# Moving an input check into the first layer and two output tiles behind the second projection

## The chip, the cores and the metric

The kernel runs on one core of a Trainium2 chip. The metric is the time of one execution on the device in microseconds. A core has five engines with a queue each: PE (matrix multiplications; PEld is its loading of weights), DVE (vector), ACT (scalar and activation), POOL, and SP, which issues the DMA transfers here. Each engine works through its own instructions in the order in which the program issued them, and waits where an instruction needs another engine's result.

## The reference, cut to what matters

Attention over 4 batches, 8 heads, 768 positions and 64 features a head, with 8 global keys, a window of 96 and a bias that falls with distance, is followed by a soft mixture of 8 experts with 4 slots each:

```python
logits = x @ phi                                  # x: 3072 x 512, 32 slots
d = softmax of logits over the tokens             # dispatch
slot_input = (d.T @ x).reshape(E, 4, 512)
h = np.maximum(slot_input[e] @ w1[e], 0.0)        # first layer, 8 experts
slot_out[e] = h @ w2[e]                           # second layer
c = softmax of logits over the slots              # combine
return c @ slot_out                               # 3072 x 512
```

## The kernel before, in words

The kernel is made for inputs with certain properties (sizes of the window, no score sum too small, and others). It computes on the fast path, and beside it a flag that says whether the inputs had them; at the very end every engine loads the flag, and only if it is set a general version (`general`) computes all again.

The attention part follows an order written out by hand (the list `ORDER`) and ends near 140 us. Everything here is about what comes after it. There, too, the program text is the order: inside `manual_schedule` each engine runs its instructions as the text issues them. The stages are:

- `last_dispatch` and `slots` finish the slots' inputs.
- `moe.hidden(…, 0, …)` is the first layer for experts 0 to 3 (PE L124); in its midst `between` sets up `fl` and makes the token softmax of the combine weights on DVE and ACT (L870 to L169).
- A loop over `a` in 0, 1: for `a == 0` it splits two batches' combine weights into two 16-bit parts (`split`, ACT L177 and DVE L178) and issues loads of the second layer's weights (`load_w`, SP L410); for `a == 1` it runs the first layer for experts 4 to 7 and issues the last loads.
- `hidden_t` transposes both results (PE L138, copies ACT L142 and DVE L144). `by_slot` turns the combine weights so that slots lie on partitions (PE L188, copies ACT L192 and DVE L194).
- `project(n, a, cs)` is the second layer (PE L154) for the output's column half `n`, the experts of group `a` and some chunks `cs`. `slots_out(n)` finishes it on DVE (L199, L200).
- `combine(n, t0, sizes)` makes output tiles of 128 tokens and 256 columns for half `n` (PE L214), in pairs: a pair is copied out of PSUM by ACT (L217) or by DVE (L219) in turn, and each group of `sizes` is sent by SP (L220), from one of eight buffers (`obs`) used in turn.

The first half's 24 tiles are interleaved with the second half's projection; the second half's 24 come at the end. `check_inputs` stands between the first half's last combine and the rest of the second projection. It is a transpose of `xmax` on PE (L891) and 13 small DVE operations that write columns of `fl` (L885 to L899). `set_flag` is a matmul with one column that sums the verdicts over the partitions (PE L903) and one DVE operation that writes `flag` (L904). PSUM tiles come from `LeftBanks.tile`, which goes round six banks.

Of the kernel before, what the change touches and what calls it, by code (L numbers as in the profile page):

```python
# [80 lines left out]
class Moe:  # L81
# [117 lines left out]
        nc.vector.tensor_scalar(out=oh, in0=o, scalar1=self.sgn[:, 0:1], scalar2=None, op0=ALU.mult)  # L199
        nc.vector.scalar_tensor_tensor(out=sot, in0=o, scalar=self.sgn[:, 1:2], in1=oh.bitcast(F32), op0=ALU.mult, op1=ALU.add)  # L200

    def combine(self, ps, ct, n, sot, obs, out, t0, sizes):


        nc = self.nc
        at, w = OUT_PART[n]
        for size in sizes:
            obs.append(obs.pop(0))
            ob = obs[-1][:, 0:w * size]
            for m in range(0, size, 2):  # L210
                cp = ps.tile([P, 512], F32, name="cp", tag="x")
                for k in range(2):
                    t = t0 + m + k
                    nc.tensor.matmul(out=cp[:, w * k:w * k + w], lhsT=ct[:, t * P:t * P + P], rhs=sot, start=True, stop=True)  # L214
                dst = ob[:, m * w:m * w + 512]
                if (t0 + m) // 2 % 2 == 0:
                    nc.scalar.copy(out=dst, in_=cp)  # L217
                else:
                    nc.vector.tensor_copy(out=dst, in_=cp)  # L219
            nc.sync.dma_start(  # L220
                out=out[P * t0:P * (t0 + size), at:at + w].rearrange("(t p) f -> p t f", p=P), in_=ob.rearrange("p (t f) -> p t f", f=w))
            t0 += size
# [75 lines left out]
def tile_attention_moe(ctx: ExitStack, tc: tile.TileContext, qk, v, phi, w1, w2, nn, out):  # L298
# [22 lines left out]
    moe = Moe(tc, ident, sgn, const.tile([P, P], F16, name="ident16"))  # L321
# [64 lines left out]
    for k, n in enumerate(held):  # L386
        at = 0
        for c0, c1 in sorted((c0, c1) for sp in spaces for h, c0, c1 in sp if h == n) + [(WP, WP)]:
            if at < c0:
                extras.append((NW + k, at, c0))  # L390
            at = c1
    places += places[0:5] + places[8:8 + 27 - npl]

    def piece(k):
        m, r = divmod(k, 16)
        if m == 0:
            a, r = divmod(r, 8)
            half, s = divmod(r, 4)
        else:
            half, r = divmod(r, 8)  # L400
            a, s = divmod(r, 4)
        return m, 4 * a + s, half
# [3 lines left out]
    def load_w(pieces, c0=0, c1=WP):  # L406

        for k in pieces:
            m, e, half = piece(k)
            nc.sync.dma_start(out=places[k][:, c0:c1], in_=(w1, w2)[m][e][:, WP * half + c0:WP * half + c1])  # L410
# [445 lines left out]
    left = LeftBanks()  # L856
# [21 lines left out]
    ct = ts.tile([P, B * S], F32R, name="ct")  # L878
    ohs = ts.tile([P, HF], F32R, name="ohs")
    sots = ts.tile([P, DM], F32R, name="sots")  # L880

    def check_inputs():

        def reduced(c, rows, x, axes, at_least):
            nc.vector.tensor_reduce(out=fl[0:rows, c:c + 1], in_=x, axis=axes, op=ALU.min)  # L885
            nc.vector.tensor_scalar(out=fl[0:rows, c:c + 1], in0=fl[0:rows, c:c + 1], scalar1=at_least, scalar2=None, op0=ALU.is_ge)

        reduced(1, KB, rsall[:, :, 0:6], AX.XY, RS_MIN)
        reduced(6, TN[6], rsall[0:TN[6], :, 6], AX.X, RS_MIN)
        xt = left.tile([P, 512], F32, name="xt", tag="x")  # L890
        nc.tensor.transpose(out=xt[0:B * H, 0:KB], in_=xmax, identity=ident[0:KB, 0:KB])  # L891
        nc.vector.tensor_reduce(out=fl[0:B * H, 5:6], in_=xt[0:B * H, 0:KB], axis=AX.X, op=ALU.max)
        nc.vector.tensor_scalar(out=fl[0:B * H, 5:6], in0=fl[0:B * H, 5:6], scalar1=X_MIN, scalar2=None, op0=ALU.is_ge)
        reduced(7, KB, cst[:, :, 1], AX.X, 0.5)
        nc.vector.tensor_scalar(out=fl[:, 2:3], in0=nlo, scalar1=1.0, scalar2=None, op0=ALU.is_ge)
        nc.vector.tensor_scalar(out=fl[:, 3:4], in0=nlo, scalar1=float(WIN), scalar2=None, op0=ALU.is_le)
        nc.vector.tensor_scalar(out=fl[:, 4:5], in0=ngl, scalar1=float(NG), scalar2=None, op0=ALU.is_le)
        nc.vector.tensor_reduce(out=fl[:, 8:9], in_=fl[:, 0:8], axis=AX.X, op=ALU.min)
        nc.vector.tensor_scalar(out=fl[:, 9:10], in0=fl[:, 8:9], scalar1=-1.0, scalar2=-1.0, op0=ALU.add, op1=ALU.mult)  # L899

    def set_flag():
        ft = left.tile([P, 512], F32, name="ft", tag="x")
        nc.tensor.matmul(out=ft[0:1, 0:1], lhsT=fl[:, 9:10], rhs=ones[:, 0:1], start=True, stop=True)  # L903
        nc.vector.tensor_scalar(out=flag[0:1], in0=ft[0:1, 0:1], scalar1=0.5, scalar2=None, op0=ALU.is_ge)  # L904
# [3 lines left out]
    def split(b):  # L908
        moe.split(lnat[:, 8 * b:8 * b + NJ], sps[b % 2])
# [4 lines left out]
    for a in range(2):  # L914
        if a == 1:
            moe.hidden(left, Moe.slot_view(sl), lambda e, half: wt[0, e, half], a, hss[a])
        if a == 0:
            split(0)
            split(1)
            for c in (0, WP // 2):  # L920
                load_w(range(npl, 28), c, c + WP // 2)
        else:
            for c in range(0, WP, WP // 4):
                load_w(range(28, 32), c, c + WP // 4)
    for a in range(2):
        moe.hidden_t(left, hss[a], hts[a])
    for b in (0, 1):
# [3 lines left out]
    obs = [places[16 + i // 2][:, 4 * HF * (i % 2):4 * HF * (i % 2) + 4 * HF] for i in range(8)]  # L931
    ops = [left.apart(n) for n in range(2)]

    def project(n, a, cs=range(8)):
        moe.project(ops[n], hts[a], lambda e, h: wt[1, e, h], n, a, cs)

    def slots_out(n):
        at, w = OUT_PART[n]
        moe.slots_out(ops[n][:, 0:w], ohs[:, 0:w], sots[:, at:at + w])

    def combine(n, t0, sizes):
        at, w = OUT_PART[n]
        moe.combine(left, ct, n, sots[:, at:at + w], obs, out, t0, sizes)

    project(0, 0)
    project(0, 1)
# [1 line left out]
    project(1, 0, range(2))  # L948
    by_slot(2)
    combine(0, 0, (2, 2, 4))  # L950
    project(1, 0, range(2, 4))
    combine(0, 8, (4,))
    project(1, 0, range(4, 5))
    by_slot(3)
    project(1, 0, range(5, 6))
    combine(0, 12, (4,))
    project(1, 0, range(6, 8))
    combine(0, 16, (4,))
    project(1, 1, range(2))
    combine(0, 20, (4,))  # L960
    check_inputs()
    project(1, 1, range(2, 8))
    slots_out(1)
    set_flag()
    combine(1, 0, (2, 2) + (4,) * 5)
    order.close()
    tail.close()
# [206 lines left out]
```

## Time and profile before

| | us |
|---|---|
| median of 3 runs | 204.69 |
| lowest and highest | 204.19, 205.63 |
| the profiled execution | 206.07 |
| its span in the trace | 204.3 |

| engine | busy, us | share of the span |
|---|---|---|
| PE | 181.1 | 89% |
| DVE | 150.9 | 74% |
| ACT | 128.4 | 63% |
| POOL | 113.7 | 56% |

The profile gives, for one execution, when each instruction ran, on which engine, and what ended the idle time in front of it. A row of the order of time has the start, the length, the engine, the line of the kernel, the operation, the tile written and the tile read, shapes, a count (xN merges instructions in a row), and in brackets the idle time before it and what ended it. Starts count from the beginning of the span. A row of a stage has the busy time of each engine in that stretch. The engines overlap the end of one instruction with the start of the next, so that neighbours can overlap by some hundredths of a microsecond.

### The profile page before, as it was taken

Reading aid. Unit: us, or ns where it says so; the run is one execution under the profiler, and the core shown is the slowest. Engines: PE = TensorE matmul, PEld = TensorE weight load, DVE = VectorE, ACT = ScalarE, POOL = GpSimd, SP = SyncE. Lnnn points to the kernel's source line nnn. Section 1 sums busy time; section 2 is a strip of 40 time slices with the busy share of each in tenths; the row PEclk is TensorE's granted clock in tenths of the full one; section 3 lists DMA queues with packets and bytes.
Section 4 is the critical chain, followed back from the end, with each engine's and each line's share of the span. In section 5 each row is a group of like instructions: output and inputs, shape, how many; then the busy total and the mean of one; then the engine's idle time right before and its main releaser. Section 6 shows DMA issues by size and latency. Waiting matters only on the chain. (4 is left out here: it accounts for less than half of the span.)

```text
span 204.3 us, 6475 instructions
## 1 busy us (share of the span) xinstructions
PE 181.1 (89%) x2646; PEld 130.4 (64%) x2646; DVE 150.9 (74%) x379; ACT 128.4 (63%) x177; POOL 113.7 (56%) x139
## 2 busy tenths in 40 slices
PE   8879899999899999999999999988799999997400
PEld 2348687888697878878878777766343366654400
DVE  3986999899989779979878999994718670546700
ACT  2318699996899878979799989954200580431500
POOL 7362769999989996998889989730000000000000
PEclk9975999999999999999999999999999999999955
DMA  3948999999999997283584876879999999997791
GB/s 97 417 163 310 363 338 397 368 382 380 341 395 377 315 391 243 52 355 95 188 305 147 274 265 198 328 242 377 373 413 405 407 398 341 344 360 239 237 344 58
DMA packets 21095, 61.40 MB, mean 301 GB/s; under 512 B 2368, under 2 KB 9408, under 8 KB 19392
## 3 DMA queue, kind: packets, MB, share of 16 engines
q1 hardware_dynamic: 20912, 60.89, 82.3%
q8 instruction: 23, 0.38, 0.7%
q14 instruction: 16, 0.13, 0.2%
q10 hardware_dynamic: 144, 0.00, 0.0%
HBM read 54.59 MB, written 6.29 MB: 298 GB/s over the span
## 5 line engine op out<-in xcount | busy, mean ns | idle before, releaser
L595 POOL TENSOR_TENSOR wa<-wa 128x432 f16<-128x432 f32 x88 | 96.1, 1120 | 18.2 <-ACT wa L587 17.2
L547 PE MATMUL sc<-wa 64*128 64x216 f32 (+2 forms) x448 | 50.3, 357 | 1.4 <-DVE mx L557 1.4
L587 ACT CAST wa<-wa 128x1296 f16<-128x1296 f32 x32 | 40.6, 1268 | 7.8 <-PE x L611 6.5
L611 PE MATMUL x<-wa 128*128 128x65 f16 (+1 forms) x1248 | 43.8, 193 | 0.7 <-issue 0.4
L547 PEld LDWEIGHTS sc<-wa 64*128 64x128 f32 x448 | 39.3, 198 | 8.0 <-issue 3.9
L611 PEld LDWEIGHTS <-wa 128*128 128x128 f16 x1248 | 40.1, 97 | 6.0 <-issue 4.6
L577 ACT ACTIVATE wa<-wa,nb 128x1296 f32<-128x1296 f32 x32 | 43.5, 1374 | 0.5
L557 DVE CUSTOM_DVE_ANT_1 wa<-sc,wa,mx 128x864 f32<-128x864 f32 x32 | 35.7, 1115 | 5.8 <-PE sc L547 3.5
L557 DVE CUSTOM_DVE_ANT_1 wa<-sc,wa 128x864 f32<-128x864 f32 x16 | 16.8, 1050 | 3.2 <-POOL wa L595 1.8
L628 DVE CUSTOM_DVE_ANT_1 xn<-x,rc 120x448 f32<-120x448 f32 x24 | 14.9, 623 | 0.9 <-PE m L745 0.2
L536 DVE SCALAR_TENSOR_TENSOR wa<-wa 128x896 f16<-128x896 f32 x11 | 15.1, 1374 | 0.0
L645 ACT COPY wa<-m 128x480 f32<-128x480 f32 (+1 forms) x30 | 13.5, 475 | 2.1 <-PE m L640 2.1
L640 PE MATMUL m<-ident,xn 120*128 120x120 f32 x77 | 12.0, 277 | 0.0
L217 ACT COPY wa<-cp 128x512 f32<-128x512 f32 x12 | 6.5, 599 | 8.2 <-PE cp L214 8.1
L531 ACT ACTIVATE wa<-wa 128x896 f16<-128x896 f32 x8 | 7.6, 950 | 6.1 <-DMA wa<-in_v_dram 5.1
L124 PE MATMUL hp<-wp,sl 128*32 128x512 f32 x96 | 10.7, 594 | 0.7 <-DVE sl L111 0.4
L219 DVE COPY wa<-cp 128x512 f32<-128x512 f32 x12 | 7.7, 687 | 4.7 <-PE cp L214 3.8
L670 PE MATMUL m<-wa,phis 128*32 128x240 f32 (+1 forms) x128 | 9.0, 332 | 0.2 <-ACT wa L645 0.2
L640 PEld LDWEIGHTS m<-ident,xn 120*128 120x128 f32 x77 | 7.8, 140 | 1.7 <-ACT nb L574 0.5
L165 ACT ACTIVATE lnat<-lnat 120x1024 f32<-120x1024 f32 x1 | 1.1, 1057 | 12.1 <-DVE lnat L164 12.1
L564 PE MATMUL m<-ident,mx 128*1 128x128 f32 x32 | 6.3, 278 | 2.7 <-DVE mx L557 2.0
L154 PE MATMUL a<-wp,wa 128*32 128x256 f32 x128 | 8.3, 384 | 0.0
(170 smaller groups left out, 220.5 us busy)
## 6 DMA issues: line engine op xcount, KB each, us to landing
wa<-in_qk_dram SPq DMA_DIRECT2D x15, 832.0 KB, 6.7
wp<-in_w_dram SPq DMA_DIRECT2D x12, 1024.0 KB, 8.0
out_dram<-wa SPq DMA_DIRECT2D x10, 512.0 KB, 5.1
wa<-in_v_dram SPq DMA_DIRECT2D x11, 448.0 KB, 4.1
wp<-in_w_dram SPq DMA_DIRECT2D x8, 512.0 KB, 10.2
wp<-in_w_dram SPq DMA_DIRECT2D x16, 256.0 KB, 5.3
wp<-in_v_dram SPq DMA_DIRECT2D x5, 448.0 KB, 6.2
wa<-in_w_dram SPq DMA_DIRECT2D x3, 432.0 KB, 5.6
```

The lines of the kernel that those rows point to most:

```text
L124: nc.tensor.matmul(out=hp[n][32 * s:32 * s + 32, :], lhsT=slv(a, c, s), rhs=w1(e, c // 2)[:, (c % 2) * DF + 512 * n:(c % 2) * DF + 512 * n ...
L536: nc.vector.scalar_tensor_tensor(out=vlo[k].rearrange(flat), in0=raw_v(u).rearrange(flat), scalar=V_SC, in1=vhi[k].rearrange(flat)[:, :, 0 ...
L547: nc.tensor.matmul(out=sc[:, i, at:at + n], lhsT=r_[r, KCOL[j]:KCOL[j] + KR], rhs=r_[r, KW + KB * j:KW + KB * j + n], start=True, stop=True)
L557: nc.vector.tensor_tensor_reduce(out=tbs[u % NTB].rearrange("p (i c) -> p i c", i=2)[:, :, BW * k:BW * k + BW], in0=scs.pop((u, k))[:, :, ...
L577: nc.scalar.activation(out=head(u, i), in_=head(u, i), func=AF.Exp, bias=nbs[u], scale=T_SC)
L587: nc.scalar.copy(out=h, in_=t)
L595: (engine or nc.gpsimd).tensor_tensor(out=w, in0=t, in1=h, op=ALU.subtract)
L611: nc.tensor.matmul(out=x[:, (D + 1) * t:(D + 1) * t + d], lhsT=w[:, c:c + P], rhs=vv[:, j, i, 0:d], start=(z == 0), stop=(z == len(ops) - ...
L628: nc.vector.tensor_tensor_reduce(out=xnb[(u // 2) % 3][:, :, c:c + D], in0=out_of(u, i)[:, :, 0:D], in1=rcs.pop((u, i)).unsqueeze(2).to_br ...
L640: nc.tensor.transpose(out=m[:, at:at + KB], in_=xnb[(u // 2) % 3][:, t, P * (p % 2):P * (p % 2) + P], identity=ident[0:KB, 0:KB])
L645: nc.scalar.copy(out=xtb[u % 3][:, a:a + n], in_=ms.pop((u, k))[:, 0:n])
L670: nc.tensor.matmul(out=ms[u][32 * s:32 * s + 32, 0:n], lhsT=phis[:, units[u - k][1], :], rhs=xtb[(u - k) % 3][:, SW * s:SW * s + n], start ...
```

## The change

Three edits, all behind the attention part. `check_inputs()` moves from behind the first half's combine into the loop, behind the two splits of `a == 0`, and so ahead of the loads there and of the first layer for experts 4 to 7. `set_flag()` moves from behind `slots_out(1)` to the place right behind the loop, ahead of `hidden_t`. The first half's last combine makes 2 tiles instead of 4; the other 2 are made behind `slots_out(1)`, with their copy on ACT (by the old rule it would be on DVE), and sent on their own.

```diff
-    def combine(self, ps, ct, n, sot, obs, out, t0, sizes):
+    def combine(self, ps, ct, n, sot, obs, out, t0, sizes, act=False):
...
-                if (t0 + m) // 2 % 2 == 0:
+                if act or (t0 + m) // 2 % 2 == 0:
                     nc.scalar.copy(out=dst, in_=cp)
...
         if a == 0:
             split(0)
             split(1)
+            check_inputs()
             for c in (0, WP // 2):
                 load_w(range(npl, 28), c, c + WP // 2)
         else:
             for c in range(0, WP, WP // 4):
                 load_w(range(28, 32), c, c + WP // 4)
+    set_flag()
     for a in range(2):
         moe.hidden_t(left, hss[a], hts[a])
...
     project(1, 1, range(2))
-    combine(0, 20, (4,))
-    check_inputs()
+    combine(0, 20, (2,))
     project(1, 1, range(2, 8))
     slots_out(1)
-    set_flag()
+    combine(0, 22, (2,), True)
     combine(1, 0, (2, 2) + (4,) * 5)
```

More of the change, by code (lines that the diff above doesn't have):

```diff
@@ L939, in slots_out, with combine @@
         moe.slots_out(ops[n][:, 0:w], ohs[:, 0:w], sots[:, at:at + w])
-    def combine(n, t0, sizes):
+    def combine(n, t0, sizes, act=False):
         at, w = OUT_PART[n]
-        moe.combine(left, ct, n, sots[:, at:at + w], obs, out, t0, sizes)
+        moe.combine(left, ct, n, sots[:, at:at + w], obs, out, t0, sizes, act)
     project(0, 0)
```

## The prediction

> **What bounds the kernel now.** I read the stages first, then the order of the last 20 us, then the stretch around 164 us, where the moved work lands. Columns of the stage rows: stretch, its length, busy time (and instructions) of PE, PEld, DVE, ACT, POOL, then the granted clock, the DMA share and GB/s.
>
> ```profile
> 165.00:170.00 5.00, 5.00 (x81) 3.61 (x83) 3.30 (x6) 2.99 (x6) 0.00 (x0) 1.00 1.03 389
> 170.00:175.00 5.00, 5.00 (x97) 2.79 (x89) 0.72 (x2) 0.00 (x0) 0.00 (x0) 1.00 0.97 332
> 175.00:180.00 5.00, 5.00 (x62) 3.08 (x58) 3.13 (x6) 2.78 (x5) 0.00 (x0) 1.00 1.01 346
> ...
> 188.50:189.00 0.50, 0.50 (x6) 0.50 (x6) 0.06 (x1) 0.30 (x1) 0.00 (x0) 1.00 0.00 0
> ...
> 190.50:191.00 0.50, 0.50 (x6) 0.43 (x5) 0.50 (x2) 0.50 (x2) 0.00 (x0) 1.00 0.97 317
> ...
> 196.00:198.00 2.00, 0.00 (x0) 0.00 (x0) 0.00 (x0) 0.00 (x0) 0.00 (x0) 0.50 1.04 341
> ```
>
> From 165 to 180 us PE has no idle time at all (5.00 of 5.00), and this lasts to the end of the second projection. DVE and ACT are half idle there. DMA is full too, but then it stands empty around 188.5 and is full again from 190.5: it waited for the first tiles of the second half. So up to 187 us PE's order of work sets the time, and behind it a drain of the second half's 3.1 MB at about 340 GB/s, which starts when the first tiles are there. The order at that border:
>
> ```profile
> 186.90 0.11 PEld L903 LDWEIGHTS ft<-ones,fl 128*1 128x1 f32 x2 [0.47 <-issue]
> 186.93 0.19 PE L903 MATMUL ft<-ones,fl 128*1 128x1 f32 x2
> 186.99 0.48 DVE L199 TENSOR_SCALAR ohs<-a,sgn 128x256 fp32r<-128x256 f32 x1 [0.20 <-PE a L154]
> 187.51 0.48 DVE L200 SCALAR_TENSOR_TENSOR sots<-a,sgn,ohs 128x256 fp32r<-128x256 f32 x1
> 187.91 0.13 DVE L904 TENSOR_SCALAR flag<-ft 1x1 int32<-1x1 f32 x1
> 188.10 3.08 PEld L214 LDWEIGHTS cp<-sots,ct 128*128 128x128 f32 x24 [1.09 <-issue]
> 188.14 3.25 PE L214 MATMUL cp<-sots,ct 128*128 128x256 f32 x24 [1.01 <-DVE flag L904]
> 188.70 3.03 ACT L217 COPY wa<-cp 128x512 f32<-128x512 f32 x6 [4.23 <-PE cp L214]
> ...
> 189.32 6.83 SPq L220 DMA_DIRECT2D out_dram<-wa  x7
> ```
>
> The reader sees a chain: projection ends, DVE makes the slots' outputs (L199, L200, to 187.99), PE combines, ACT copies, SP sends at 189.32. DVE had waited 0.20 us for PE at 186.99, so the check ahead of it in DVE's queue, as it stands, holds up nothing. What a microsecond of PE is worth before 187 us is a microsecond at the end.
>
> **What goes from the old place.** The check's rows there, with PE's weight loads around the last combine of the first half:
>
> ```profile
> 181.68 0.53 PEld L214 LDWEIGHTS cp<-sots,ct 128*128 128x128 f32 x4 [0.41 <-issue]
> ...
> 182.34 0.59 PEld L154 LDWEIGHTS a<-wp,wa 128*32 128x32 f32 x16
> ...
> 183.35 0.53 PEld L214 LDWEIGHTS cp<-sots,ct 128*128 128x128 f32 x4 [0.41 <-issue]
> 183.82 0.10 PEld L891 LDWEIGHTS xt<-ident,xmax 120*32 120x32 f32 x1
> ...
> 184.12 2.32 PEld L154 LDWEIGHTS a<-wp,wa 128*32 128x32 f32 x48 [0.20 <-issue]
> 184.12 2.80 PE L154 MATMUL a<-wp,wa 128*32 128x256 f32 x48
> 184.12 0.69 DVE L219 COPY wa<-cp 128x512 f32<-128x512 f32 x1 [0.91 <-PE cp L214]
> 184.73 0.34 DVE L885 TENSOR_REDUCE fl<-rsall 120x1 f32<-120x192 f32 x1
> ...
> 186.63 0.15 DVE L899 TENSOR_SCALAR fl<-fl 128x1 f32<-128x1 f32 x1
> ```
>
> Four tiles and the return to the projection take 0.66 us (181.68 to 182.34); with the transpose of xmax (L891) 0.77 (183.35 to 184.12). The transpose is worth 0.11. The four tiles' loads take 0.47 (183.35 to 183.82), two of them 0.23. PE gets to the end of the projection **0.34 us** earlier (bounds 0.2 and 0.5, by what the hand-over between the two kinds of matmul keeps of it). The 13 DVE operations go from a place where they cost nothing.
>
> The two tiles come back behind the projection. There PE waits from 187.12 to 188.10 for L199 and L200, and two matmuls (0.23) with their hand-over lie inside that wait. ACT is idle before 188.70 (4.23 us of idle in its row): its one copy, a sixth of the 3.03 in that row or about 0.6 with the overlap, runs from 0.6 behind the projection's end to 1.2 behind it (188.14 to 188.70 is the lag from matmul to copy), that is 187.5 to 188.1 in the old times. The extra 256 KB are issued at about 188.1, 1.2 us ahead of the first send of the second half; at 341 GB/s they are 0.77 us of a DMA that stands empty then. I cost this at nothing. If that cover were gone, it is 0.77 us at most, the queue's time in front of the second half. The buffers are used in turn, eight of them, and the reused ones come one send nearer; the nearest reuse is still seven sends apart.
>
> **What comes in at the new place.** The check follows the second split (L177/L178) on DVE, and `set_flag` stands ahead of both `hidden_t`. Rows of that place:
>
> ```profile
> 163.57 0.62 DVE L178 TENSOR_TENSOR sp<-lnat,sp 120x448 f16<-120x448 f32 x1
> 163.63 0.61 PE L124 MATMUL hp<-wa,sl 128*32 128x512 f32 x4
> 164.17 1.97 PE L138 MATMUL htp<-ident,wp 128*128 128x128 f32 x16
> 165.30 0.69 DVE L144 COPY wa<-htp 128x512 f32<-128x512 f32 x1 [1.11 <-DMA wp<-in_w_dram]
> 165.98 1.15 PE L188 MATMUL ctp<-ident,sp 120*128 120x120 f16 x14
> 167.06 7.11 PE L154 MATMUL a<-wa 128*32 128x256 f32 x128
> ```
>
> DVE is free after the second split at 164.19. It was late already, since the token softmax and its exponential stand in front. The check took from 184.81 (end of the copy before it) to 186.78, that is 1.97 us, so it now ends at 164.19 + 1.97 = 166.16. PE has finished the first layer at 164.24 and, in its order, must now run L903, which reads the check's result. It waits. Behind it in PE's queue stand the 16 transposes L138, the 14 matmuls L188 and the whole projection, so everything waits with it. From DVE's end to PE's weight load I take 0.11 (L200's end 187.99 to 188.10): load at 166.27, matmul at 166.30. For the step from a one-column matmul to the next kind the trace has L570 ahead of L547:
>
> ```profile
> 22.14 0.35 PE L570 MATMUL m<-mm,bsel 2*128 2x1 f32 x2
> 22.42 1.07 PE L547 MATMUL sc<-wa 64*128 64x216 f32 x12
> ```
>
> 0.28 us. The first transpose starts at 166.58 instead of 164.17: **2.41 us** later. Bounds: 2.1 when the hand-overs come to nothing, 2.7 when the 13 operations no longer overlap (their rows sum to 2.3 instead of 1.97). The transpose of xmax ahead of the first layer's second half (0.11) vanishes in this wait. L904 follows on DVE and waits for L903, to about 166.7; the next DVE step, L144, needs transposes that end at about 167.7, so nothing more is lost. From there to the projection PE had no gap before (L138, L188, L154 follow without one), so it cannot catch up. SP's weight loads wait for the readers in the first layer, at most 0.11 later. POOL only has the flag to read at the end.
>
> **Sum.** + 2.41 - 0.34 = **+2.07 us**, at the projection's end and, since the drain hangs on it, at the end. The profiled execution took 206.07 us with a span of 204.3; I expect a span near 206.4. On the median of the runs shown, 204.69, that is **206.8**. Own range of this case: 1.6 (2.1 - 0.5) to 2.5 (2.7 - 0.2), so 206.3 to 207.2.
>
> **Rivals.**
>
> *PE's clock falls in the new gap.* PE's longest gap ahead of the clock's first fall, and rows on a grid of the clock's changes:
>
> ```profile
> 10.66 1.08 PE L547 MATMUL sc<-wa 64*128 64x216 f32 x12 [1.40 <-DVE mx L557]
> ...
> 9.78:13.19 3.41, 1.60 (x14) 1.04 (x14) 3.11 (x7) 1.28 (x1) 3.25 (x3) 1.00 0.30 68
> 13.19:16.60 3.41, 3.30 (x16) 2.30 (x18) 2.60 (x3) 0.40 (x2) 0.66 (x1) 0.50 0.85 306
> 16.60:20.02 3.42, 3.42 (x24) 3.31 (x22) 1.90 (x5) 3.39 (x3) 0.90 (x1) 0.50 0.97 368
> 20.02:23.43 3.41, 3.16 (x31) 2.22 (x29) 3.30 (x7) 2.44 (x4) 2.81 (x4) 1.00 0.87 291
> ...
> 142.90:146.31 3.41, 2.22 (x21) 0.88 (x18) 2.75 (x17) 1.51 (x6) 0.00 (x0) 1.00 1.04 369
> ...
> 190.68:194.10 3.42, 0.71 (x5) 0.43 (x4) 1.94 (x4) 1.05 (x3) 0.00 (x0) 1.00 0.95 307
> 194.10:197.51 3.41, 0.00 (x0) 0.00 (x0) 0.00 (x0) 0.00 (x0) 0.00 (x0) 0.50 1.04 337
> ```
>
> The clock fell at 13.19 and 194.10 and rose at 20.02; all three lie on one grid of 3.41 us. It fell behind a stretch with 1.60 us of PE work and stayed behind one with 2.22. The new gap runs from 164.35 to about 166.58, 2.2 us; a stretch of the grid that holds all of it has 1.2 us of work, less than the one that fell. By where the grid lies, one holds 1.8 us of idle time or more in some 6 of 10 executions ((3.41 - 2.2 + 0.8) / 3.41). Then one stretch at half clock costs 1.7 us of a PE without slack: 206.8 + 1.7 = 208.5, and 210.2 if, as at 13.19, it takes two. Against it: that early stretch's matmuls used 64 rows, this one's all 128; one fall is little to set a threshold by. Chance 0.33. The Trainium skill (TensorE: Matmul & The Clock Gate, "Why this matters for your kernels") allows idle gaps up to about 3 us before the clock halves. By that rule a gap of 2.2 us leaves the clock alone and the sum stays as forecast; the fall at 13.19, with a longest gap of 1.40 us ahead of it, speaks against the rule.
>
> *The wait costs nothing (not slower).* If weights arrived so late that the projections were paced by them, a PE that comes 2.4 us later would find them all there and catch up. The decisive point: PE's waits for `wp` behind 167 us would have to sum to 2.4 us. Only the 0.34 would be left, 204.4, or as much as 205 with part of the wait. For it: DMA is full to 187 us. Against it: PE has 5.00 of 5.00 in all three rows above. Chance 0.06.
>
> *The extra send is in the way.* With the first half's sends 2 us later, the 256 KB may still be in the queue when the second half starts: 0.4 to 0.77 more, 207.2 to 207.6. Against it: 1.2 us of lead and an empty DMA. Chance 0.09.
>
> **How the numbers follow.** Forecast 0.52 (206.3 to 207.2), clock 0.33, no cost 0.06, send 0.09. A measurement here can tell about 1%, 2.05 us, so slower begins at 206.74, in the midst of the forecast's own range: its 0.52 is split about evenly, 0.24 above and 0.28 within. Slower: 0.24 + 0.33 + 0.08 = 0.65; within 1%: 0.31; faster by over 1% needs a gain of which the trace has no row: 0.04, out of the free wait's share. Range 205.8 to 209.0: it holds the forecast, the send and the clock with one stretch, and leaves out the free wait and a clock down for two.
>
> **What would show it.** In the changed kernel's trace: L899 ending near 166.2 and a PE wait of about 2 us on it ahead of L903; the first L138 near 166.6; L154 solid from 169.5 to 189; L199 near 189.1 with no DVE work before it; one ACT copy and a send of 256 KB ahead of the first of the second half, near 190.2; first send of that half near 191.4. The granted clock between 164 and 175 decides on the first rival. I am wrong if the transposes start near 164.3, which would mean that the check ran earlier on DVE than its place in the order says, or if PE shows waits for weights behind 169 us.

## The result, and the profile after

The changed kernel took 207.38 us in the median of 4 runs (206.79 to 208.12), beside 205.0 for the kernel before: a ratio of 1.0134, 95% interval 1.0095 to 1.0173, or 2.7 us; the medians are 2.4 apart. One profiled execution below, of the kernel before with 15 sends, was a disturbed one (209.08 us, where the other twelve runs of that kernel took at most 206.55): only the length of its closing is used, and such runs are left out of every comparison.

First, what the two profiled spans (204.3 and 206.1) do not say. They differ by 1.8 us only, because the two executions began differently: the granted clock was at half for a different length of time. Stage rows of the kernel before, then of the changed one (columns as in the prediction; the granted clock is the third number from the end):

```profile
13.00:20.00 7.00, 6.70 (x36) 5.59 (x38) 4.67 (x9) 3.76 (x4) 1.72 (x2) 0.51 0.90 331
```

```profile
13.00:20.00 7.00, 6.11 (x42) 4.99 (x42) 5.43 (x11) 4.46 (x5) 2.45 (x3) 0.76 0.90 333
...
163.50:165.10 1.60, 0.00 (x0) 0.00 (x0) 1.35 (x12) 0.60 (x1) 0.00 (x0) 1.00 1.02 405
191.75:192.50 0.75, 0.35 (x3) 0.14 (x2) 0.75 (x2) 0.74 (x2) 0.00 (x0) 1.00 0.07 14
```

Between 13 and 20 us the clock was at half nearly all the time before (0.51), and for half of it after (0.76). The two splits on DVE, which lie ahead of the moved check, start at 161.89 (first row of the fence after the next) instead of 163.03:

```profile
163.03 1.16 DVE L178 TENSOR_TENSOR sp<-lnat,sp 120x448 f16<-120x448 f32 x2 [0.63 <-ACT sp L177]
```

That is 1.14 us that the change has nothing to do with. So times below count from the splits' start. The second row of the second fence is PE's gap, with the clock at 1.00; the third is a hole in the drain, which the prediction did not have.

Order of time of the changed kernel around the moved check:

```profile
161.89 1.16 DVE L178 TENSOR_TENSOR sp<-lnat,sp 120x448 f16<-120x448 f32 x2 [0.63 <-ACT sp L177]
162.97 0.34 DVE L885 TENSOR_REDUCE fl<-rsall 120x1 f32<-120x192 f32 x1
...
164.87 0.15 DVE L899 TENSOR_SCALAR fl<-fl 128x1 f32<-128x1 f32 x1
165.39 0.15 DVE L904 TENSOR_SCALAR flag<-ft 1x1 int32<-1x1 f32 x1 [0.37 <-PE ft L903]
...
159.84 3.62 PE L124 MATMUL hp<-wa,sl 128*32 128x512 f32 x32
165.16 0.19 PE L903 MATMUL ft<-ones,fl 128*1 128x1 f32 x2 [1.71 <-DVE fl L899]
165.28 1.97 PE L138 MATMUL htp<-ident,wp 128*128 128x128 f32 x16
167.09 1.15 PE L188 MATMUL ctp<-ident,sp 120*128 120x120 f16 x14
168.17 7.11 PE L154 MATMUL a<-wa 128*32 128x256 f32 x128
```

The reader sees the forecast wait by name: L903 waited 1.71 us for L899, and the transposes, the slot matmuls and the projection followed without a gap. The end of the projection and the drain:

```profile
187.75 0.48 DVE L199 TENSOR_SCALAR ohs<-a,sgn 128x256 fp32r<-128x256 f32 x1 [3.43 <-PE a L154]
...
188.21 0.59 ACT L217 COPY wa<-cp 128x512 f32<-128x512 f32 x1 [2.63 <-PE cp L214]
...
188.82 0.37 SPq L220 DMA_DIRECT2D out_dram<-wa  x1
190.07 0.37 SPq L220 DMA_DIRECT2D out_dram<-wa  x1
190.54 1.61 SPq L220 DMA_DIRECT2D out_dram<-wa  x1
192.26 0.41 SPq L220 DMA_DIRECT2D out_dram<-wa  x1
```

The extra send goes at 188.82, the first of the second half at 190.07. The second send of that half then takes 1.61 us to issue, where the ones around it take 0.4, and the DMA stands nearly empty from 191.75 to 192.50. While that send is issued, a 16 KB transfer of the instruction queue q8 is under way, called an instruction fetch below. In the kernel before the same send took 0.97:

```profile
189.78 0.97 SPq L220 DMA_DIRECT2D out_dram<-wa  x1
```

And the closing, from SP's first semaphore of the last wait to the end of the span. Rows of SP by line, of the kernel before, then of the changed one (first and last start behind the durations):

```profile
L972 SPq EVENT_SEMAPHORE  x8: 17/17/17, 201.7 to 202.3; - x8
L1170 SPq DRAIN  x3: 7/7/28, 202.8 to 204.0; - x3
```

```profile
L973 SPq EVENT_SEMAPHORE  x8: 17/17/17, 202.9 to 203.4; - x8
L1171 SPq DRAIN  x3: 7/7/127, 205.1 to 205.6; - x3
```

Before, 201.7 to 204.3 is 2.6 us; after, 202.9 to 206.1 is 3.2 (these rows give starts to 0.1 us, so a closing is good to about 0.1). SP's first DRAIN comes 0.5 us behind its last semaphore before and 1.7 after. That pause is moved rather than added: the DRAINs spread over 1.2 us before and over 0.5 after, so before, two of them lie ahead of the pause, and after, all three behind it. In both kernels an 8 KB transfer of the instruction queue q14 starts 0.6 us behind the first semaphore (202.3 and 203.5), ahead of the pause.

So the 2.94 us between the two traces, counted from the splits (1.8 + 1.14), are: first send of the second half 28.18 behind the splits' start instead of 26.29, **1.89** from PE's wait; from that send to the closing 12.8 instead of 12.4, **0.4** in the drain; closing **0.6**. Each is read from one execution of each kernel.

### The profile page after: what moved, and what is told of

Read it like the earlier page. It is cut to its first block, busy times and chain, and to the rows that moved or that the text cites. A ratio compares the mean times of both kernels' runs of the same rounds, so it can differ in the third digit from the quotient of the medians.

```text
span 206.1 us, 6475 instructions
## 1 busy us (share of the span) xinstructions
PE 179.9 (87%) x2646; PEld 129.4 (63%) x2646; DVE 150.9 (73%) x378; ACT 129.2 (63%) x178; POOL 113.8 (55%) x139
## 4 chain that ended last, share of the span: by engine, by line
PE 60%; DVE 16%; ACT 10%; issue 4%; DMA 2%; POOL 2%; DVEq 0%; ACTq 0%
PE sc L547 15%; PE x L611 15%; PE a L154 7%; PE m L640 5%; ACT wa L587 4%; ACT wa L577 4%; PE m L670 3%; PE cp L214 3%; DVE wa L557 2%; DMA nraw<-in_n_dram 2%; PE m L570 2%; PE m L564 2%; POOL wa L595 2%; PE hp L124 2%; DVE wa L595 2%
## 5 line engine op out<-in xcount | busy, mean ns | idle before, releaser
L547 PE MATMUL sc<-wa 64*128 64x216 f32 (+2 forms) x448 | 49.3, 351 | 2.4 <-DVE mx L557 1.5
L547 PEld LDWEIGHTS sc<-wa 64*128 64x128 f32 x448 | 38.4, 193 | 8.8 <-issue 4.2
L536 DVE SCALAR_TENSOR_TENSOR wa<-wa 128x896 f16<-128x896 f32 x11 | 15.9, 1446 | 0.0
L217 ACT COPY wa<-cp 128x512 f32<-128x512 f32 x13 | 7.0, 598 | 7.3 <-PE cp L214 7.2
L219 DVE COPY wa<-cp 128x512 f32<-128x512 f32 x11 | 7.0, 686 | 3.8 <-PE cp L214 3.8
L214 PE MATMUL cp<-sots,ct 128*128 128x256 f32 x48 | 7.6, 298 | 0.8 <-ACT wa L217 0.8
```

The lines of the kernel that those rows point to most:

```text
L536: nc.vector.scalar_tensor_tensor(out=vlo[k].rearrange(flat), in0=raw_v(u).rearrange(flat), scalar=V_SC, in1=vhi[k].rearrange(flat)[:, :, 0 ...
L547: nc.tensor.matmul(out=sc[:, i, at:at + n], lhsT=r_[r, KCOL[j]:KCOL[j] + KR], rhs=r_[r, KW + KB * j:KW + KB * j + n], start=True, stop=True)
```

## The experiments

Each ratio is against runs of the kernel before in the same session. "At equal clock" below gives us against the kernel before, with the start of the kernel taken out: least squares over the executions of all sessions, with a constant for each kernel and one common slope on the mean granted clock (-0.8 us for each 0.01); the uncertainty is one standard error, the scatter of 0.52 us over the root of the number of runs. A send is said to stand for as long as SP takes to issue it. The changed kernel stands at +2.7 ± 0.26 by it.

**Check and flag alone.** The change with the four tiles put back where they were; check and flag stay where the change has them.

```diff
-    combine(0, 20, (2,))
+    combine(0, 20, (4,))
-    combine(0, 22, (2,), True)
```

> The check and the flag move as in the change; the tiles stay as before (four in the first half's last combine, none behind the projection). Theory A (PE waits for the check ahead of the transposes, and in the drain the second send stands behind an instruction fetch): PE's wait shifts the projection's end by 2.25 us less 0.11 for the transpose of xmax, +2.14; the fetch keeps its place in PE's stream, so the drain may lose anything from 0 to 1.05 more: 2.1 to 3.2 over before. Theory B (the extra send of 256 KB is what holds up the drain): no hole, +2.1, with the second send of the second half issued in under 1 us.

Ratio 1.0132 (1.0082 to 1.0181); at equal clock +2.3 ± 0.21. The second send took 0.79 and the closing 2.4 us. The check and the flag alone cost nearly all of it. The first send of the second half comes 28.43 behind the splits' start, 2.14 more than before, which is theory A's term for PE; from there to the closing it is 13.0, 0.6 more than before, though no extra send is there. Theory B's number for the time fits here too, so the time alone does not part the two.

**Tiles alone.** The change with check and flag put back.

```diff
-            check_inputs()
-    set_flag()                        # ahead of hidden_t
     combine(0, 20, (2,))
+    check_inputs()
     project(1, 1, range(2, 8))
     slots_out(1)
+    set_flag()
     combine(0, 22, (2,), True)
```

> The two tiles move as in the change; check and flag stay where they were before. Theory A: PE gets to the projection's end about 0.28 us earlier, nothing waits, so -0.3 against before unless a fetch falls on the second send. Theory B: the same -0.3 and then the drain's hole of 1.05 on top, +0.8.

Ratio 1.003 (0.9996 to 1.0064); at equal clock +0.5 ± 0.15. Neither number: the second send stood 1.16 us, and the closing took 3.2. This run put the closing on the list: at equal clock the tiles, forecast to gain 0.3, lose.

**The flag alone put back.** The change with `set_flag()` behind `slots_out(1)`.

```diff
-    set_flag()                        # ahead of hidden_t
...
     slots_out(1)
+    set_flag()
     combine(0, 22, (2,), True)
```

> The change with the flag's matmul and its DVE step alone back behind the second projection; the check stays in the first layer. Theory A: PE no longer waits for the check; the 13 DVE steps delay the copies L144 by 0.9 us, which costs PE at most 0.2 ahead of the first projection, so -0.4 + 0.2 = -0.2 against before. The rival (the check's DVE time is what costs, not the flag's place): at least +1 against before. Theory B: +0.8 by the extra send.

Ratio 1.0028 (0.9997 to 1.0059); at equal clock +0.7 ± 0.15. The 2 us go when the flag alone is put back, though the 13 DVE steps stay in the first layer. Its rows:

```profile
158.99 3.62 PE L124 MATMUL hp<-wa,sl 128*32 128x512 f32 x32
162.54 1.97 PE L138 MATMUL htp<-ident,wp 128*128 128x128 f32 x16
164.34 1.15 PE L188 MATMUL ctp<-ident,sp 120*128 120x120 f16 x14
165.42 0.85 PE L154 MATMUL a<-wa 128*32 128x256 f32 x12
```

PE goes from the first layer to the transposes without a gap, and the delayed copies (the two L144 run one behind the other from 164.21) cost it nothing. What is over is not PE's: the first send of the second half comes 26.28 behind the splits' start (161.05), as before (26.29). The third of a microsecond that PE gains further on is used up ahead: the first layer ends later, so the transposes start 1.49 behind the splits' start instead of 1.14. This kernel too has 15 sends and a closing of 3.2, and its second send stood 1.85. I expected -0.2; the drain and the closing are what I missed.

**The fetch moved.** In the changed kernel, 20 matmuls of one column ahead of the flag's.

```diff
         ft = left.tile([P, 512], F32, name="ft", tag="x")
+        for _ in range(20):
+            nc.tensor.matmul(out=ft[0:1, 8:9], lhsT=busy_in[:, 0:1], rhs=busy_in[:, 0:1], start=True, stop=True)
```

> The change with 20 matmuls of one column put ahead of the flag's matmul, inside PE's wait of 1.7 us, so that they cost nothing; they move every later instruction of PE's stream by 40 places, and with it the places where PE's instructions are fetched. Theory A: the fetch no longer meets the second send, that send is issued in under 0.6 us, the drain has no hole and the time falls by about 1.0 against the change (1.9 over before). Theory B, or a hole with another cause: as the change, 2.4 to 2.9 over before.

Ratio 1.0121 (1.0077 to 1.0165); at equal clock +2.2 ± 0.21. In the changed kernel the fetch of q8 started between 190.4 and 190.5 (read from the DMA view in slices of 0.1 us), as the second send was about to be issued, and ended near 191.7; here it starts between 187.1 and 187.2. The sends:

```profile
189.94 0.37 SPq L220 DMA_DIRECT2D out_dram<-wa  x1
190.41 0.42 SPq L220 DMA_DIRECT2D out_dram<-wa  x1
190.93 0.44 SPq L220 DMA_DIRECT2D out_dram<-wa  x1
```

0.42 instead of 1.61, and no hole (DMA share 1.02 between 191.75 and 192.50): the stand of the second send moves with PE's instruction stream, and theory B is out, since the extra send is still there. The gain was half of what I expected, 0.5 (206.1 to 205.6 with the split at the same time): SP's first closing semaphore then came 2.4 us behind the time at which the DMA share falls under a half (200.2) instead of 1.7 (201.2); why is open. The Trainium skill (Runtime: NRT & Kernel Launch, "Instruction fetch mechanics") says that an engine's instructions are refilled in blocks of 16 KB, 256 instructions, and counts the refill as mostly hidden; size and movement agree, hidden it was not.

**14 sends instead of 15.** The change with two sends for the first eight tiles.

```diff
-    combine(0, 0, (2, 2, 4))
+    combine(0, 0, (4, 4))
```

> The change with the first three sends of the first half made two (groups of 4 and 4 tiles instead of 2, 2 and 4), so that SP issues 14 sends in all, as before the change, instead of 15. Theory A2 (the one more wait and send in SP's stream move the place of its last instruction fetch, and the closing of the kernel takes 3.1 us from SP's first closing semaphore to the end instead of 2.5): that stretch is 2.4 to 2.6 us again and the time falls by about 0.6 against the change, to 1.8 to 2.3 over before. Rival (the closing is longer because the flag's branch or the drain is later): still 3.0 to 3.2 us, and the time as the change, 2.4 to 2.9 over before.

Ratio 1.007 (1.0036 to 1.0104); at equal clock +2.1 ± 0.16, 0.6 ± 0.3 less than the change; by the ratios it is 1.3 less. SP's closing:

```profile
L973 SPq EVENT_SEMAPHORE  x8: 17/17/17, 201.8 to 202.4; - x8
L1171 SPq DRAIN  x3: 7/7/28, 202.9 to 204.0; - x3
```

201.8 to the end at 204.2 is 2.4, with the flag's branch, the wait and the extra send as in the change: the forecast of A2, and its rival is out. The stretch from the first send of the second half (189.56) to the closing is 12.3 here, 0.5 shorter than in the change, so the difference in time is not the closing's alone.

**Tiles alone with 14 sends** (the same edit on the kernel with only the tiles moved).

> Only the tiles moved (check and flag where they were before), again with groups of 4 and 4 for the first eight tiles, 14 sends in all. Theory A2: the 0.6 of the closing goes, and what is left is PE's gain of 0.28 against what the second send stands behind an instruction fetch: -0.3 to +0.3 against before. Rival: as with 15 sends, +0.6 to +0.8.

Ratio 0.9993 (0.9959 to 1.0026); at equal clock -0.1 ± 0.15, against +0.5 with 15 sends; closing 2.3. The second send stood 1.66 here, and a fetch fell on it.

**Tiles alone, 14 sends, fetch moved** (that, and the 20 matmuls).

> The kernel with only the tiles moved and 14 sends, and 20 matmuls of one column ahead of the flag's matmul, in PE's wait behind the second projection; they move the fetch of PE's instructions away from the second send of the last half. Theory A with A2: the second send is issued in under 0.6 us, the drain has no hole, -0.3 to -0.8 against before, the only version under it. If the hole has another cause: as without the 20 matmuls.

Ratio 0.9949 (0.992 to 0.9979): 204.28 beside 205.26, faster than both kernels. At equal clock -0.5 ± 0.16.

```profile
187.99 0.37 SPq L220 DMA_DIRECT2D out_dram<-wa  x1
188.79 0.37 SPq L220 DMA_DIRECT2D out_dram<-wa  x1
189.26 0.54 SPq L220 DMA_DIRECT2D out_dram<-wa  x1
```

Second send 0.54, closing 2.5: both losses are gone, and PE's quarter of a microsecond is kept (the first send of the second half 26.05 behind the splits' start, for 26.29).

**The check made twice**, in the changed kernel.

```diff
             check_inputs()
+            check_inputs()
```

> The change with the check's operations made twice at the new place, so that DVE is done 1.97 us later. If PE's wait for DVE sets the time with nothing behind it: PE's wait grows from 1.7 to about 3.6 us, and the time by 2.0 over the change, 4.4 to 4.9 over before. The rival of the prediction (PE's clock falls in the gap): with a gap of 3.6 us the granted clock is at half for 3.4 us behind it, and the time grows by 3.7 over the change, 6 or more over before.

Ratio 1.0265 (1.0228 to 1.0303), 5.2 between the medians and 2.5 over the change, between the two forecasts (equal clock can't be used, as the fall below is part of the mean clock). Rows of its stages, and of PE, DVE and the first projection:

```profile
13.00:20.00 7.00, 5.60 (x50) 4.17 (x50) 6.42 (x14) 4.47 (x5) 2.45 (x3) 1.00 0.91 341
...
163.75:167.16 3.41, 1.15 (x14) 0.99 (x11) 2.17 (x16) 0.78 (x2) 0.00 (x0) 1.00 1.03 387
...
167.20:170.40 3.20, 3.20 (x23) 2.91 (x21) 1.80 (x3) 1.72 (x4) 0.00 (x0) 0.50 0.81 277
170.80:172.00 1.20, 1.20 (x24) 0.72 (x28) 1.20 (x3) 0.78 (x2) 0.00 (x0) 1.00 1.00 341
```

```profile
157.69 2.78 PE L124 MATMUL hp<-wp,sl 128*32 128x512 f32 x24 [1.11 <-ACT wp L128]
...
160.92 1.16 DVE L178 TENSOR_TENSOR sp<-lnat,sp 120x448 f16<-120x448 f32 x2 [0.63 <-ACT sp L177]
...
166.17 0.19 PE L903 MATMUL ft<-ones,fl 128*1 128x1 f32 x2 [2.26 <-DVE fl L899]
166.29 2.91 PE L138 MATMUL htp<-ident,wp 128*128 128x128 f32 x16
168.99 1.80 PE L188 MATMUL ctp<-ident,sp 120*128 120x120 f16 x14
170.72 1.50 PE L154 MATMUL a<-wa 128*32 128x256 f32 x24
```

The clock did fall, to 0.50 from 167.2 to 170.4, behind a stretch of 3.41 us with 1.15 us of PE work and a longest gap of 2.26. The 16 transposes took 2.91 us instead of 1.97, the slot matmuls 1.80 instead of 1.15. The first projection starts 9.80 behind the splits' start instead of 6.28: 3.52 more, of which 1.98 is DVE's second check (L903 5.25 behind instead of 3.27) and 1.54 the clock. That is the rival's 3.7, not the 2.0 without it. The spans differ by only 2.6 (208.7 and 206.1) because this execution's clock did not fall at the start (1.00 between 13 and 20). So the event of the first rival is shown, in one execution, and close by: at the very gap that the prediction had reckoned with for the change. The gap grew by 0.55 only, as PE came later too: the first layer waited 1.11 us for ACT (L128), which fits one tile more in the round of six banks but was not shown.

What decides a fall stays open. The prediction measured it by PE's work in a stretch of the grid; rows of the changed kernel on its grid (the clock fell at 15.54):

```profile
12.13:15.54 3.41, 1.95 (x15) 1.28 (x16) 3.41 (x5) 0.10 (x1) 1.64 (x2) 1.00 0.76 259
...
162.32:165.73 3.41, 1.70 (x18) 0.69 (x11) 2.64 (x16) 1.20 (x3) 0.00 (x0) 1.00 1.02 405
```

It fell behind 1.95 us of work, most of it matmuls of 64 rows, and stayed behind 1.70, the stretch with the new gap. So work in a stretch does not decide it alone, and neither does the length of a gap: the prediction's rows show a fall behind a longest gap of 1.40, and there was none here behind one of 1.71. The Trainium skill (TensorE: Matmul & The Clock Gate, "Why this matters for your kernels") asks for no idle gaps over some 3 us; in the check made twice the clock fell behind one of 2.26, so the rule allows too much here.

**The kernel before with the fetch moved** (the 20 matmuls alone).

> The kernel before with the 20 matmuls of one column ahead of the flag's matmul, and nothing else: tiles, check and flag as before. If the gain of the best version so far (-1.0) came from moving the fetch of PE's instructions: the second send of the last half is issued in under 0.6 us instead of 0.97, and -0.4 to -0.9 against before. If it came from the two tiles: no change, within 0.3.

Ratio 1.0001 (0.9968 to 1.0034); at equal clock +0.1 ± 0.15. The second send took 0.43 instead of 0.97, and nothing came of it: the DMA was full without a break sooner, and SP's first closing semaphore came 2.5 us behind the fall of the DMA share (199.0) instead of 1.7 (200.0), much as with the fetch moved in the change. So a send freed from a fetch isn't always worth its stand, and the best version's gain isn't the fetch alone.

**The kernel before with 15 sends.**

```diff
-    combine(0, 20, (4,))
+    combine(0, 20, (2, 2))
```

> The kernel before with the last send of the first half, 4 tiles, made as two sends of 2, in the same place: 15 sends in all, nothing else changed. Theory A2 (the closing depends on the number of instructions in SP's stream): from SP's first closing semaphore to the end 3.0 to 3.2 us instead of 2.6, and +0.6 against before. Rival (the closing is longer where the extra send lies between the halves): no change, within 0.3.

Ratio 1.0023 (0.9985 to 1.0061); at equal clock +0.7 ± 0.15. The closing took 3.0 us. By the ratio alone it can't be told from nothing; with the start taken out, and with the closing's length, one send more costs about 0.6, in the first half here as between the halves in the tiles alone.

## Why the prediction was right or wrong

- **The wait: right, with one size off.** L899 ended 1.97 behind the end of the splits (163.05 to 165.02), as worked out; PE's load came 0.11 behind it, as worked out. The step to the first transpose was 0.12 (165.16 to 165.28), not the 0.28 taken from L570. The shift against the splits was 2.25, not 2.41. Putting the flag back took the whole of it away; the check's DVE time alone cost PE nothing.
- **PE's gain: right.** From the first transpose to L199, 22.47 instead of 22.82: 0.35 for 0.34 forecast. Net 1.89 at the first send, for 2.07.
- **The extra send: wrong, in the step "I cost this at nothing".** Its data did go through the empty DMA ahead of the second half (it was issued 1.25 us ahead of it, 1.2 forecast). But it is one more item in SP's stream, and with 15 sends the closing took 3.0 to 3.2 in all six kernels profiled, with 14 it took 2.3 to 2.6 in all six, the kernel before among them: some 0.6 that no row of before could price.
- **The drain: not in the sum.** The second send stood behind an instruction fetch already before (0.97); after, 1.61. The stretch from the first send to the closing grew by 0.4. The stand does not explain this by itself: with check and flag alone it was 0.79 and the stretch 13.0, and with the fetch moved in the kernel before 0.43 and 12.8, both longer than the 12.4 of before. So what sets that stretch is in part open.
- **The rivals.** The clock stayed at 1.00. The gap, from the first layer's end to the first transpose, was 1.82 (163.46 to 165.28; 1.71 to the flag's matmul) and not 2.2: 0.16 by the shorter step, the rest because PE reached it later against DVE than I reckoned, 0.35 instead of 0.11 (163.46 against the split's end at 163.05, before 164.25 against 164.19). The stretch of the grid that holds it had 1.70 us of work and not 1.2. The fall was real and near; the work in a stretch, by which I gave it its chance, does not order the falls seen. The free wait is out: no wait for weights behind 168 us, PE solid. The send in the way was right in its size and wrong in its mechanism: its data had the DMA to itself, and what it cost came at the closing.
- **The time.** 2.07 was forecast; 1.9 of wait, 0.6 of closing and some 0.2 to 0.4 of drain were measured. The median of 207.38 lies above the 206.3 to 207.2 that the forecast's own terms allowed, and within the wider range that was to hold the rivals as well, though neither the clock nor a collision in the queue brought it there: that part is luck. The direction and most of the size come from the wait, which was foreseen.

What stays open: why SP's closing depends on the number of sends (a fetch of SP's own instructions fits the transfer of q14 ahead of SP's pause, but was not shown), what sets the stretch from the first send to the closing beyond the second send, what delays the closing semaphore where that send was freed, and what decides a fall of the clock.

## What to carry to other kernels

Work moved off a busy path into idle time of its engine can still be waited for: ask of each moved step when its last input is ready there, and put the instruction that consumes it (here one matmul and one DVE step) where the engine waits anyway. A gap on PE is also a risk for its clock: one of 2.26 us halved it here, one of 1.71 did not. Differences under 1 us at the end of a kernel may come from where instruction fetches and the last sends fall, so change those alone before crediting an edit.

## What the runs showed of the hardware

- In nine of the twelve kernels a 16 KB instruction transfer of q8 was under way when the second or the third send of the second half began. In each, that send ended 0.3 to 0.4 us behind the transfer's end and took 0.8 to 1.9 us; in the other three the second send took 0.42 to 0.54. In the change the DMA behind it ran empty (0.07 of its share from 191.75 to 192.50); 40 more instructions on PE's queue moved the transfer and ended the stand. Not every send that meets one is held: with the fetch moved in the kernel before, a send of the first half took 0.37 at 178.56, inside such a transfer.
- One send more in SP's stream lengthened the closing from 2.3 to 2.6 us to 3.0 to 3.2.
- The granted clock halved for 3.4 us behind a PE gap of 2.26 us in the one execution that had it, and not behind one of 1.71. In one trace it fell behind a stretch of its grid with 1.95 us of PE work and stayed behind one with 1.70.
